# One list of steps for the first block of a fused chunk attention and Mish feed-forward kernel

## The chip, the core and the metric

The kernel runs on one NeuronCore of a Trainium2 chip. The metric is device time in microseconds (us). The kernel before takes 855.69 us (median of 3 runs, 854.79 to 856.61).

The engines that matter here: PE (TensorE, matrix products into PSUM), ACT (ScalarE, tables, copies and casts), DVE (VectorE, arithmetic on tensors), and SP (SyncE, whose queue issues nearly all transfers). Each engine takes its own instructions strictly in the order in which the program states them, and waits on semaphores for the others.

## The reference

```python
# attention, apart for each chunk of 64 positions; q, k, v: (8 batch, 8 heads, 576, 64)
scores = (q_c @ k_c.T) / sqrt(64)
attn   = exp(scores - max(scores))
attn   = attn / (sum(attn) + 1e-9)
x      = (attn @ v_c)                 # -> (4608 tokens, 512)
# feed-forward
h   = x @ w_in                        # 512 -> 2048
g   = h * tanh(log1p(exp(min(h, 20))))   # Mish
out = g @ w_out                       # 2048 -> 512
```

The two weights come as 64-bit floats; a matrix product in single precision is made here of products of a rounded upper part ("hi") and a rest ("lo").

## The kernel before, in words

The 4608 tokens are 36 tiles of 128. The first block holds four of them (two "pairs" of tiles, 512 tokens); the other 32 follow in four groups of four pairs (m = 1 to 4). These groups use products of sums of sub-matrices; their operands are 256 KB pieces of the weights, kept in DRAM. Only the first block works with the weights as they come in. It has to do four things at once:

- **Attention of its own tokens** (pairs 0 and 1), in halves of one tile: scores (`a_scores`, PE), `a_max`, `a_sub` (DVE), `a_exp` (ACT), `a_inverse` and `a_norm` (DVE), `a_transpose` (PE), `a_copy` (ACT), `a_values` (PE), and the split of the result into hi and lo (`a_hi` on ACT, `a_lo` on DVE, tile `x_first`).
- **Attention of the next group** (pairs 2 to 5), the same steps on whole pairs; `a_raw` (ACT) keeps the result, and `x_step` (ACT and DVE) makes the split operands of the group m = 1 of it.
- **The weights.** There are 19 loads: 0 to 5 bring one row of 128 columns (0.5 MB of doubles), 6 to 18 bring two (1 MB). Below, "load n" is the transfer (L102), "scale n" its two ACT steps (L114, L119), "bits n" its two DVE steps (L132), "hi n" the ACT cast (L150) and "lo n" the DVE subtraction (L153). Even n from 6 on are `w_in` (tile `wi`), odd ones `w_out` (tile `wo`). Bits of `w_in` also go to DRAM (L136, `cs`). The tile that the loads fill (`wst`) and the tile of the scaled values (`wc`) have four places: a load of two rows takes two of them, so load n can go out when bits n-2 are done, and scale n can begin when load n has landed and lo n-2 has freed the place in `wc`.
- **The feed-forward of the block.** Slot s (0 to 15) is a strip of 128 of the 2048 hidden columns. `up s` (L461) is 12 products of 512 columns, Mish (L474, "mish s") goes to a tile `z`, `gh s` and `gl s` split it, `down s` (L493) is 12 products that add to four accumulators over all slots. Two banks hold the results of `up`, so `up s` needs mish s-2.

When both strips of a `wi` tile are there, `w_keep(u)` (L163) stores three quarters of it to DRAM, three transfers of 256 KB ("keep u", u = 0 to 7), for the products of the groups. After the last lo, `s_load`, `s_adds`, `s_hi`, `s_lo` build the four other operands of unit 0 from `cs`: they use the place of the whole `wc` tile, so they wait for lo 18, and their store (L200) must land before the third product of unit 0 can load its operand (L751).

What sets the order before: `prologue` (attention of the first tokens, loads 0 to 6, up 0 to 1) is written out by hand with loops over halves; then `slot(s)` states one slot of the feed-forward with the steps of one load, in a fixed pattern; and two small tables (`on_pe`, `beside_pe`) hang the attention of the next pairs, the x steps and the sums onto half slots. In a slot, `up s+1` comes first, then load, hi, the split of z, scale, lo, then `down s-1`, mish, bits, keep. Which casts `gh` go to ACT is in `BY_SCALAR`. The unit code of the groups follows, and reads the last two `down` groups from a list.

Of the kernel before, what the change touches and what calls it, by code (L numbers as in the profile page):

```python
# [23 lines left out]
def kernel(  # L24
# [451 lines left out]
    def g_split(d, z, name, on_scalar=False):  # L476
        d["gh"] = ew.tile([P, TOK], F32R, name=f"gh_{name}", tag="gh")
        if on_scalar:
            nc.scalar.copy(out=d["gh"], in_=z)
# [3 lines left out]
        nc.vector.tensor_tensor(out=d["gl"], in0=z, in1=d["gh"].bitcast(F32), op=ALU.subtract)
# [5 lines left out]
    def down_mm(key, f, d, t, n):  # L489
        if f == 0 and n == 0:  # L490
            acc[t] = ps_o.tile([P, DM], F32, name=f"o_{key}_{t}", tag=f"o{t}")
        g, part = ((d["gl"], 0), (d["gh"], 1), (d["gh"], 0))[n]
        nc.tensor.matmul(  # L493
            acc[t],
            lhsT=g[:, t * P : (t + 1) * P],
            rhs=wo[:, f, part],
            start=(f == 0 and n == 0),
            stop=(f == NF - 1 and n == 2),
        )
# [118 lines left out]
    on_pe, beside_pe = {}, {}
    for i, (h0, h1) in enumerate(((2, 8), (10, 15), (17, 22), (24, 28))):
        j = first_pair(1) + i  # L620
        for n, step in ((0, a_scores), (h1 - h0, a_transpose), (h1 - h0 + 1, a_values)):
            on_pe.setdefault(h0 + n, []).append((step, j))
        for n, steps_ in (
            (0, (load_v,)),
            (1, (a_max, a_sub)),
            (2 - (i == 3), (a_exp,)),
            (3 - (i == 3), (a_inverse,)),
            (4 - (i == 3), (a_norm,)),
            (h1 - h0, (a_copy,)),
            (h1 - h0 + 1, (a_raw,)),  # L630
        ):
            beside_pe.setdefault(h0 + n, []).extend((step, j) for step in steps_)
        if i:
            beside_pe.setdefault(h0 - 6, []).append((lambda j: load_qk(j, pool=(xo_p, "x")), j))
    for s, half, steps_ in (
        (19, 0, (0,)),
        (20, 0, (1,)),
        (21, 0, (2,)),
        (22, 0, (3, 4)),
        (27, 0, (5, 6)),  # L640
        (28, 0, (7, 8)),
        (29, 0, (9, 10)),
        (30, 1, (0, 1)),
        (31, 1, (3, 4, 2, 5, 7)),
    ):
        beside_pe.setdefault(s, []).extend((lambda n, half=half: x_step(1, half, n), n) for n in steps_)

    beside_pe[27].append((s_adds, 0))
    beside_pe[28].append((s_hi, 0))
    beside_pe[29].insert(0, (s_lo, 0))  # L650
    beside_pe[30].append((s_load, 1))

# [4 lines left out]
    BY_SCALAR = (1, 3, 5, 7, 8, 10, 12, 14)  # L657

    def slot(s):
        n = s + SINGLE - 1  # L660
# [9 lines left out]
        if s == 1:  # L670
            w("lo", now)
        w("scale", 5 if s == 0 else n + 1)
        if s == 0:
            w("bits", 4)
        if s != 1:
            w("lo", now)
        run(beside_pe, 2 * s)

        if s < NF - 1:
            filled()  # L680
        down(0, s, it[s])
        run(on_pe, 2 * s + 1)
        if s + 1 < NF:
            it[s + 1]["z"] = z_tile(f"z_{s + 1}")
            mish(it[s + 1]["z"], it[s + 1]["h"])
        if s == 0:
            w("hi", 4)
            w("bits", 5)
            w("load", SINGLE + 1)
            w("lo", 4)  # L690
            w("scale", SINGLE)
            w("bits", SINGLE)
        elif s == 1:
            w("hi", n)
            w("lo", n)
# [5 lines left out]
        if s == NF - 3:
            s_load(0)
            load_op()
            load_op()
        run(beside_pe, 2 * s + 1)
        if s == NF - 2:
# [494 lines left out]
```

## Time and profile before

| | |
|---|---|
| median of 3 runs | 855.69 us |
| profiled execution, its time | 854.58 us |
| its span, first to last instruction | 852.8 us |
| granted TensorE clock, mean | 0.988 |
| up 1 ends, up 2 begins on PE | 31.6 us |
| down 14 begins (the last `down` before unit 0) | 142.6 us |
| third product of unit 0 (first with an operand built in this block) | 151.7 us |

The first block is the stretch from 0 to about 145 us. From about 190 us on PE works nearly without a pause (each 20 us from 200 to 300 us hold 20.00 us of PE work), so what the first block takes is nearly a constant ahead of the rest. A busy share is the share of time in which an engine works at all; the clock that PE is granted is shown as a number from 0 to 1; the DMA share is the mean busy share of the 16 DMA engines. In a row of the timeline or of a group, the text in brackets is how long the engine sat idle just before, and what ended that.

### The profile page before, as it was taken

The page shows a single profiled execution, that of the slowest core. Times are in us where ns is not written, and L with a number is a line of the kernel's source. Part 1 is how long each engine was busy: PE and PEld are TensorE (multiplying, and loading weights), DVE is VectorE, ACT ScalarE, POOL GpSimd, SP SyncE. Part 2 cuts the span into 40 slices and gives each one's busy share as a digit, 9 for nine tenths or more (in the row PEclk, how much of TensorE's full clock was granted, in tenths as well). Part 3 has the DMA queues.
Part 4 walks back from the last instruction along what each step waited for, and adds up shares of the span by engine and source line. Part 5 has one row for each costly group of instructions (what it writes and reads, how often), then busy time and mean ns, then how long its engine had stood idle before and what let it go on. Part 6 is the DMA issues. An engine that isn't in the chain of part 4 may idle for free.

```text
span 852.8 us, 15933 instructions
## 1 busy us (share of the span) xinstructions
PE 810.4 (95%) x6300; PEld 686.4 (80%) x6300; DVE 521.6 (61%) x765; ACT 436.1 (51%) x640; POOL 0.7 (0%) x6
## 2 busy tenths in 40 slices
PE   4878989889999999999999999999999999999997
PEld 3756867568888888788888888877899988889997
DVE  6787889655564663665764764444788723347663
ACT  4667875444443552543543534555656534444443
POOL 0000000000000000000000000000000000000000
PEclk9988999999999999999999999999999999999999
DMA  7698883877758411788886227876567777666773
GB/s 284 238 318 291 279 282 138 263 247 268 270 204 279 111 51 57 230 286 287 258 279 212 73 99 254 301 226 184 159 164 222 216 230 195 189 195 175 209 197 88
DMA packets 96441, 181.40 MB, mean 213 GB/s; under 512 B 9072, under 2 KB 29552, under 8 KB 94320
## 3 DMA queue, kind: packets, MB, share of 16 engines
q1 hardware_dynamic: 95936, 179.74, 66.4%
q8 instruction: 50, 0.82, 0.4%
q10 hardware_dynamic: 432, 0.66, 0.2%
q14 instruction: 23, 0.19, 0.1%
HBM read 137.36 MB, written 42.99 MB: 211 GB/s over the span
## 4 chain that ended last, share of the span: by engine, by line
PE 76%; DVE 10%; DMA 5%; ACT 5%; issue 2%; SPq 1%; DVEq 0%; ACTq 0%
PE x L764 17%; PE X L1063 9%; PE v L764 9%; PE Z L1063 5%; PE y L764 5%; PE av L271 2%; DMA wst<-in_w_in 2%; PE s L271 2%; PE h L461 2%; PE o L493 2%; PE pt L339 2%; DVE wc L132 1%; PE Y L1063 1%; PE o_(1, 1)_0_2761 L493 1%; PE o_(2, 1)_0_4413 L493 1%
## 5 line engine op out<-in xcount | busy, mean ns | idle before, releaser
L764 PE MATMUL x<-x_T,w 128*128 128x512 f32 x576 | 144.7, 394 | 6.4 <-ACT zb L869 3.1
L764 PEld LDWEIGHTS x<-x_T,w 128*128 128x128 f32 x576 | 106.2, 188 | 33.3 <-ACT zb L869 4.4
L1028 ACT CAST gh<-G 128x512 fp32r<-128x512 f32 x96 | 58.8, 621 | 59.4 <-PE X L1063 32.4
L1030 DVE TENSOR_TENSOR gl<-G,gh 128x512 fp32r<-128x512 f32 x96 | 65.1, 688 | 37.3 <-ACT gh L1028 36.1
L1063 PE MATMUL X<-w,gh 128*128 128x256 f32 x512 | 72.3, 283 | 0.0
L1063 PEld LDWEIGHTS X<-w,gh 128*128 128x128 f32 x512 | 66.3, 192 | 0.2
L474 ACT ACTIVATE G<-G 128x512 f32<-128x512 f32 x48 | 30.3, 632 | 57.4 <-DVE G L776 57.4
L776 DVE TENSOR_TENSOR G<-v,G 128x512 f32<-128x512 f32 x32 | 21.9, 689 | 57.2 <-ACT G L1008 34.7
L461 PE MATMUL h<-x_first,wi 128*128 128x512 f32 (+1 forms) x204 | 49.3, 393 | 1.7 <-ACT wi L150 0.8
L764 PE MATMUL v<-x_B,w 128*128 128x512 f32 x192 | 48.8, 393 | 1.3 <-DVE zb L776 1.3
L474 ACT ACTIVATE zb<-zb 128x512 f32<-128x512 f32 x32 | 20.2, 632 | 58.0 <-DVE zb L776 58.0
L764 PE MATMUL x<-x_B,w 128*128 128x512 f32 x192 | 48.6, 394 | 0.8 <-DVE x_B L416 0.8
L764 PE MATMUL y<-x_B,w 128*128 128x512 f32 x192 | 49.1, 397 | 0.0
L764 PE MATMUL v<-x_T,w 128*128 128x512 f32 x192 | 47.6, 390 | 1.2 <-DMA w<-wa 1.2
L461 PEld LDWEIGHTS h<-x_first,wi 128*128 128x128 f32 x204 | 37.7, 195 | 10.3 <-ACT wi L150 1.2
L764 PEld LDWEIGHTS v<-x_B,w 128*128 128x128 f32 x192 | 35.5, 188 | 9.9 <-DVE zb L776 2.6
L764 PEld LDWEIGHTS v<-x_T,w 128*128 128x128 f32 x192 | 35.9, 188 | 9.3 <-issue 1.6
L1063 PE MATMUL X<-w,gl 128*128 128x256 f32 x256 | 41.8, 284 | 1.3 <-DVE gl L1030 1.2
L764 PEld LDWEIGHTS x<-x_B,w 128*128 128x128 f32 x192 | 35.2, 188 | 8.6 <-DVE x_B L416 1.2
L493 PE MATMUL o<-wo,gh 128*128 128x512 f32 x128 | 41.8, 407 | 0.3 <-DVE wo L153 0.3
L764 PEld LDWEIGHTS y<-x_B,w 128*128 128x128 f32 x192 | 35.1, 188 | 7.7
L481 DVE CAST gh<-z 128x512 fp32r<-128x512 f32 x40 | 16.9, 423 | 39.7 <-PE o_(2, 0)_3_3328 L493 20.6
(181 smaller groups left out, 1583.5 us busy)
## 6 DMA issues: line engine op xcount, KB each, us to landing
w<-wa SPq DMA_DIRECT2D x224, 256.0 KB, 3.2
w<-wb SPq DMA_DIRECT2D x112, 256.0 KB, 2.9
v<-in_v SPq DMA_DIRECT2D x16, 512.0 KB, 5.7
wa<-a SPq DMA_DIRECT2D x8, 1024.0 KB, 4.3
wb<-t SPq DMA_DIRECT2D x8, 1024.0 KB, 5.0
wst<-in_w_out SPq DMA_DIRECT2D x7, 1024.0 KB, 6.5
wst<-in_w_in SPq DMA_DIRECT2D x6, 1024.0 KB, 6.0
wa<-wi SPq DMA_DIRECT2D x24, 256.0 KB, 3.7
```

The costliest lines, as they stand in the source:

```text
L132: nc.vector.scalar_tensor_tensor(out=c, in0=x, scalar=mask, in1=y, op0=op, op1=ALU.bitwise_or)
L271: nc.tensor.matmul(o[h * CHUNK : (h + 1) * CHUNK, c, t - ts.start, g], lhsT=l[rows, t, 2 * g + h], rhs=r[rows, t, 2 * g + h], start=True, ...
L339: nc.tensor.transpose(out=d["pt", ts.start][:, t - ts.start, g], in_=d["p"][:, t, g].rearrange("p c k -> p (c k)"), identity=ident,)
L461: nc.tensor.matmul(h[:, cols], lhsT=wi[i // 2][:, i % 2, w_, kt], rhs=x[:, x_, kt, cols], start=(n == 0), stop=(n == 3 * NK - 1),)
L474: nc.scalar.activation(out=out_, in_=in_, func=AF.Mish)
L481: nc.vector.tensor_copy(out=d["gh"], in_=z)
L493: nc.tensor.matmul(acc[t], lhsT=g[:, t * P : (t + 1) * P], rhs=wo[:, f, part], start=(f == 0 and n == 0), stop=(f == NF - 1 and n == 2),)
L764: nc.tensor.matmul(o, lhsT=t[:, w_, kt], rhs=x[x_][:, kt], start=(start and i == 0), stop=(i == 5), skip_group_check=not start,)
L776: nc.vector.tensor_tensor(out=z, in0=o, in1=z, op=ALU.add)
L1028: nc.scalar.copy(out=d["gh"], in_=g)
L1030: nc.vector.tensor_tensor(out=d["gl"], in0=g, in1=d["gh"].bitcast(F32), op=ALU.subtract)
L1063: nc.tensor.matmul(o, lhsT=d[g][:, t * P : (t + 1) * P], rhs=w_[:, part], start=(k in (0, 1, 3) and u == 0 and t % 2 == 0 and n == 0), sto ...
```

## The change

All steps of the first block now stand in one list, `ORDER`, which `first_block()` goes through from left to right; `atom()` turns a word into the call. The steps and their sizes are the same. What differs:

- the order of nearly everything, on every engine;
- the first tokens' attention interleaves its two halves, and its tiles are placed in other banks (`TOP_ATTENTION`, places `h`, `0`, `2`); load 0 and load 1 go out behind q and k of pair 1, loads 2 and 3 and `v` of pair 1 behind the first store of bits;
- `gh` and `gl` can stand apart (`g_upper`, `g_lower`), and seven casts `gh` instead of eight are on ACT;
- two `up` are stated in a row at several places (3 and 4, 7 and 8, 14 and 15), with two `down` in a row behind;
- the stores "keep u" stand behind the next load instead of ahead of it, and keep 4 comes after load 16, keep 6 after load 17, keep 5 and 7 after load 18.

```diff
-    def prologue(ps_f):
...
-        load_qk(0, None, (FIRST, SECOND), (nc.sync, nc.scalar))
-        w("load", 0)
-        load_v(0, room[0])
-        load_qk(1, (room[1], room[2]), (FIRST, SECOND))
-        w("load", 1)
-        load_v(1, room[3])
-        w("load", 2)
-        w("load", 3)
...
-    BY_SCALAR = (1, 3, 5, 7, 8, 10, 12, 14)
-
-    def slot(s):
...
-            up(s + 1, last="w")
-        run(on_pe, 2 * s)
-        if s > 0:
-            w("load", n + 2)
-        now = (3, 5, n)[min(s, 2)]
-        w("hi", now)
-        g_split(it[s], it[s]["z"], f"0_{s}", s in BY_SCALAR)
...
-            w("bits", n + 1)
-        if s % 2 == 0:
-            w_keep(s // 2)
...
+    ORDER = """
+        rooms, qk0, v0, qk1, a_scores 0 0, a_max 0 0, a_sub 0 0, a_scores 0 1, a_max 0 1,
...
+        a_inverse 0 1, a_norm 0 1, a_T 0 1, a_copy 0 0, a_V 0 0, a_copy 0 1, load 1, bits 0,
+        load 2, load 3, v1, hi 0, lo 0, a_hi 0 0, a_scores 1 0, a_V 0 1, a_hi 0 1, a_lo 0 0,
...
+        bits 5, lo 3, load 7, keep 0, mish 1, hi 4, gh 1, lo 4, hi 5, scale 6, bits 6, open,
+        fill 0, scores 0, up 2, lo 5, max 0, fill 1, mish 2, gh 2, sub 0, scale 7, bits 7,
+        load 8, load_v 0, load 9, hi 6, keep 1, hi 7, lo 6, scale 8, exp 0, lo 7, up 3, gl 1,
+        mish 3, up 4, gl 2, bits 8, load 10, inverse 0, load_qk 1, fill 2, gh 3, fill 3, norm 0,
+        gl 3, scale 9, mish 4, bits 9, load 11, hi 8, lo 8, up 5, keep 2, mish 5, T 0, copy 0,
...
+        load_v 2, raw 1, fill 8, scores 2, fill 9, mish 9, bits 14, load 16, up 10, hi 14, gh 9,
+        max 2, sub 2, gl 9, fill 10, scale 15, lo 14, ops 2, keep 4, exp 2, bits 15, load 17,
+        keep 6, load_qk 3, mish 10, up 11, gh 10, gl 10, hi 15, lo 15, fill 11, up 12,
...
+        keep 7, max 3, sub 3, exp 3, bits 18, fill 12, fill 13, gh 13, gl 13, hi 18, lo 18,
+        s_load 0, inverse 3, norm 3, up 14, up 15, mish 14, mish 15, gh 14, x 0 6, x 0 8,
...
+    BY_SCALAR = (2, 5, 7, 11, 12, 13, 14,)
+
+    def atom(name, *args):
...
+        elif name == "fill":
+            if a < NF - 1:
+                filled()
+            down(0, a, it[a])
...
+    def first_block():
+        for step in ORDER.split(","):
+            name, *args = step.split()
+            atom(name, *map(int, args))
```

In `ORDER`, "fill k" emits down k-1 and notes down k; "scores", "T", "V" with one number are the attention of the pairs 2 to 5 (numbers 0 to 3); "x h n" is step n of half h.

Three places show how instructions move. The first is SP's queue around loads 10 to 12 (the rows `wst`) of the program before; `cs` is the store of bits, `wa` the keep, `qk` and `v` are attention inputs.

```order
L136 DMA cs_118<-wc 128x1024
L163 DMA wa_100<-wi_390 128x2x256 x3
L102 DMA wst<-in_w_in 128x2x1024
L102 DMA wst<-in_w_out 128x2x1024
L136 DMA cs_119<-wc 128x1024
L163 DMA wa_101<-wi_537 128x2x256 x3
L102 DMA wst<-in_w_in 128x2x1024
```

The same place in the changed program:

```order
L136 DMA cs_118<-wc 128x1024
L102 DMA wst<-in_w_in 128x2x1024
L254 DMA qk_595<-in_q 128x2x512
L254 DMA qk_595<-in_k 128x2x512
L102 DMA wst<-in_w_out 128x2x1024
L163 DMA wa_101<-wi_544 128x2x256 x3
L136 DMA cs_119<-wc 128x1024
L102 DMA wst<-in_w_in 128x2x1024
```

Each even load now follows its store of bits directly; the three transfers of a keep follow the odd load.

The second place is DVE between bits 6 and bits 8 (L132 on 1024 elements; L153 is lo, L297 and L309 are max and sub of pair 2, L481 and L483 are gh and gl). Before:

```order
L132 SCALAR_TENSOR_TENSOR wc<-wst,wc 128x1024
L483 TENSOR_TENSOR gl_1_512<-z_447,gh_1_510 128x512
L153 TENSOR_TENSOR wo<-wc,wo 128x512
L153 TENSOR_TENSOR wi_537<-wc,wi_537 128x2x512
L132 SCALAR_TENSOR_TENSOR wc<-wc,wst 128x1024
L132 SCALAR_TENSOR_TENSOR wc<-wst,wc 128x1024
L297 TENSOR_REDUCE m_0_542<-s_0_475 128x16
L309 TENSOR_TENSOR p_544<-s_0_475,m_0_542 128x2x8x64
L481 CAST gh_2_561<-z_535 128x512
L483 TENSOR_TENSOR gl_2_563<-z_535,gh_2_561 128x512
L153 TENSOR_TENSOR wo<-wc,wo 128x2x512
```

Changed (gh and gl are now L485 and L489):

```order
L132 SCALAR_TENSOR_TENSOR wc<-wst,wc 128x1024
L153 TENSOR_TENSOR wo<-wc,wo 128x512
L297 TENSOR_REDUCE m_0_512<-s_0_465 128x16
L309 TENSOR_TENSOR p_534<-s_0_465,m_0_512 128x2x8x64
L132 SCALAR_TENSOR_TENSOR wc<-wc,wst 128x1024
L132 SCALAR_TENSOR_TENSOR wc<-wst,wc 128x1024
L153 TENSOR_TENSOR wi_544<-wc,wi_544 128x2x512
L153 TENSOR_TENSOR wo<-wc,wo 128x2x512
L489 TENSOR_TENSOR gl_1_568<-z_449,gh_1_452 128x512
L489 TENSOR_TENSOR gl_2_585<-z_530,gh_2_532 128x512
```

lo 5 moves ahead of gl 1, max and sub move ahead of bits 7, lo 6 behind it, and gl 1 comes seven instructions later, beside gl 2, whose gh has gone to ACT.

The third place is PE at the same time (L461 is up, one row of 12 products; L493 is down, of which the first accumulator of each is shown). Before, up 3, down 1, up 4, down 2:

```order
L461 MATMUL h_546<-x_first,wi_390 128x512 x12
L493 MATMUL o_0_519<-wo,gl_1_512 128x512
L493 MATMUL o_0_519<-wo,gh_1_510 128x512 x2
...
L461 MATMUL h_596<-x_first,wi_537 128x512 x12
L493 MATMUL o_0_519<-wo,gl_2_563 128x512
L493 MATMUL o_0_519<-wo,gh_2_561 128x512 x2
```

Changed, up 3, up 4, down 1, down 2 (down is now L499):

```order
L461 MATMUL h_555<-x_first,wi_400 128x512 x12
L461 MATMUL h_572<-x_first,wi_544 128x512 x12
L499 MATMUL o_0_514<-wo,gl_1_568 128x512
L499 MATMUL o_0_514<-wo,gh_1_452 128x512 x2
...
L499 MATMUL o_0_514<-wo,gl_2_585 128x512
L499 MATMUL o_0_514<-wo,gh_2_532 128x512 x2
```

up 4 has moved ahead of down 1.

More of the change, by code (lines that the diff above doesn't have):

```diff
@@ L476, in g_split, with g_upper @@
     def g_split(d, z, name, on_scalar=False):
+        g_upper(d, z, name, on_scalar)
+        g_lower(d, z, name)
+    def g_upper(d, z, name, on_scalar):
         d["gh"] = ew.tile([P, TOK], F32R, name=f"gh_{name}", tag="gh")
@@ L618 @@
[L618 to L651, printed above, removed]
@@ L655, in run @@
             step(arg)
-    BY_SCALAR = (1, 3, 5, 7, 8, 10, 12, 14)
-    def slot(s):
-        n = s + SINGLE - 1
-        if 1 <= s and s + 1 < NF:
-            up(s + 1, last="w")
-        run(on_pe, 2 * s)
-        if s > 0:
-            w("load", n + 2)
-        now = (3, 5, n)[min(s, 2)]
-        w("hi", now)
-        g_split(it[s], it[s]["z"], f"0_{s}", s in BY_SCALAR)
[L670 to L695, printed above, removed]
-            w("bits", n + 1)
-        else:
-            w("bits", n + 1)
-        if s % 2 == 0:
-            w_keep(s // 2)
[L701 to L706, printed above, removed]
-            for i in range(LOOK - 2):
-                load_op()
@@ new lines, with room, open_accumulators @@
+    A, B = slice(0, PTOK), slice(PTOK, TOK)
+    first = ExitStack()
+    ps_f = first.enter_context(tc.tile_pool(name="ps_f", bufs=1, space=bass.MemoryType.PSUM))
+    PLACES = {"h": HOME, "0": (ps_f, "o0"), "2": (ps_f, "o2")}
+    rooms = {}
+    opened = {}
+    def room(n):
+        if n not in rooms:
+            rooms[n] = xo_p.tile([P, 2, 2, H, CHUNK], F32, name=f"room_{n}", tag="x")
+        return rooms[n]
+    def open_accumulators():
+        first.close()
+        opened["o"] = ctx.enter_context(tc.tile_pool(name="ps_o", bufs=1, space=bass.MemoryType.PSUM))
@@ new lines @@
+    """
+    BY_SCALAR = (2, 5, 7, 11, 12, 13, 14,)
+    def atom(name, *args):
+        if name in TOP:
+            return TOP[name]()
+        a = args[0]
+        j = first_pair(1) + a
+        if name in TOP_ATTENTION:
+            step, places = TOP_ATTENTION[name]
+            t = args[1]
+            kw = {} if places is None else {"place": PLACES[places[a][t]]}
+            step(a, (FIRST, SECOND)[t], **kw)
+        elif name in steps:
+            steps[name](a)
+        elif name in attention:
+            attention[name](j)
+        elif name == "up":
+            up(a, last="w")
+        elif name == "gh":
+            g_upper(it[a], it[a]["z"], f"0_{a}", a in BY_SCALAR)
+        elif name == "gl":
+            g_lower(it[a], it[a]["z"], f"0_{a}")
+        elif name == "fill":
+            if a < NF - 1:
+                filled()
+            down(0, a, it[a])
+        elif name == "mish":
+            it[a]["z"] = z_tile(f"z_{a}")
+            mish(it[a]["z"], it[a]["h"])
+        elif name == "keep":
+            w_keep(a)
+        elif name == "x":
+            x_step(1, *args)
+        elif name == "ops":
+            for _ in range(a):
+                load_op()
+        else:
+            {"s_load": s_load, "s_adds": s_adds, "s_hi": s_hi, "s_lo": s_lo}[name](a)
@@ new lines @@
+    attention = {
+        "scores": a_scores,
+        "load_v": load_v,
+        "max": a_max,
+        "sub": a_sub,
+        "exp": a_exp,
+        "inverse": a_inverse,
+        "norm": a_norm,
+        "T": a_transpose,
+        "copy": a_copy,
+        "V": a_values,
+        "raw": a_raw,
+        "load_qk": lambda j: load_qk(j, pool=(xo_p, "x")),
+    }
+    def first_block():
+        for step in ORDER.split(","):
+            name, *args = step.split()
+            atom(name, *map(int, args))
@@ L1136 @@
     with tc.manual_schedule():
-        with tc.tile_pool(name="ps_f", bufs=1, space=bass.MemoryType.PSUM) as ps_f:
-            prologue(ps_f)
-        ps_o = ctx.enter_context(tc.tile_pool(name="ps_o", bufs=1, space=bass.MemoryType.PSUM))
-        for s in range(NF):
-            slot(s)
+        first_block()
         for m in range(1, BOTH_FROM):
```

103 lines of the change are left out of this document (43 added, 60 removed).

## The prediction

> **What bounds the kernel now.** I read the page first, then the stretches of the first block, then the chain of waits through it.
>
> ```profile
> PEclk9988999999999999999999999999999999999999
> ```
>
> (40 slices of 21.3 us each.) Only the first slices show a lowered clock, the sign that PE waited long. So the change is worth what it takes off the first 150 us, and the rest follows shifted.
>
> ```profile
> 0.00:31.56 31.56, 17.38 (x308) 14.59 (x308) 21.63 (x39) 17.55 (x29) 0.70 (x6) 0.95 0.70 253
> 31.56:137.60 106.04, 93.59 (x796) 74.42 (x796) 86.26 (x97) 76.67 (x87) 0.00 (x0) 0.92 0.76 269
> 64.82:124.30 59.48, 53.25 (x515) 43.56 (x516) 46.91 (x51) 46.33 (x52) 0.00 (x0) 0.91 0.83 292
> 39.60:124.30 84.70, 72.87 (x591) 57.88 (x590) 67.85 (x74) 62.26 (x69) 0.00 (x0) 0.90 0.84 296
> ```
>
> The columns are the stretch, its length, busy time of PE, of weight loading, DVE, ACT and POOL with their counts, granted clock, DMA share, GB/s. No engine is full: between 31.56 and 137.60 DVE works 86.26 of 106.04 us, DMA is at 0.76. The chain says why:
>
> ```profile
> 30.14 5.28 DMA wst<-in_w_in
> 41.51 1.13 ACT wc L114
> 52.08 1.22 DVE wo L153
> 58.34 6.37 DMA wst<-in_w_in
> 69.88 4.98 PE h L461 x12
> 137.56 6.09 DMA wa<-wi
> ```
>
> (start, duration, what.) It runs over loads 6 and 10, over ACT and DVE steps of the weights in between, and at the end over keep 7. Each engine waits in turn for the others. What PE pays:
>
> ```profile
> 21.40 0.63 PE L339 MATMUL pt<-ident,p 128*128 128x128 f32 x4 [2.98 <-ACT wst L119]
> 24.18 1.99 PE L271 MATMUL av<-ps,room 64*64 64x64 f32 x64
> 31.58 3.01 PE L461 MATMUL h<-x_first,wi 128*128 128x512 f32 x12 [0.26 <-ACT z L474]
> 52.31 0.77 PE L493 MATMUL o<-wo,gl 128*128 128x512 f32 x1 [4.17 <-DVE gl L483]
> 57.72 2.90 PE L461 MATMUL h<-x_first,wi 128*128 128x512 f32 x12
> 67.89 1.98 PE L271 MATMUL av<-ps,v 64*64 64x64 f32 x64 [3.37 <-ACT ps L349]
> 69.81 5.05 PE L461 MATMUL h<-x_first,wi 128*128 128x512 f32 x12
> 84.17 2.88 PE L461 MATMUL h<-x_first,wi 128*128 128x512 f32 x12
> 115.50 1.94 PE L339 MATMUL pt<-ident,p 128*128 128x128 f32 x8 [3.16 <-DVE p L330]
> 142.58 0.50 PE L493 MATMUL o<-wo,gl 128*128 128x512 f32 x1
> ```
>
> The row at 31.58 is up 2, the last one the start of down 14. From one to the other PE has 14 up and 14 down, at 2.72 us when warm (start to next start around 84.17), and four attentions at about 3.0: 88.2 us of work in 111.0. The excess is 22.8 us. Stalls of 3.2 to 4.2 us are each followed by a slow group: 12 products in 5.05 us instead of 2.88.
>
> **The change, part by part.** Work is the same but for one `gh` that moves from ACT to DVE, so every term is a shift of a wait. I walk the new order by hand with these durations:
>
> ```profile
> L132 DVE SCALAR_TENSOR_TENSOR wc<-wst,wc 128x1024 uint32<-128x1024 uint32 x13 | 15.9, 1225 | 0.4
> L114 ACT ACTIVATE wc<-wst 128x1024 f32<-128x1024 f32 x13 | 14.9, 1145 | 6.4 <-DMA wst<-in_w_in 3.7 <-DVE wo L153 2.8
> L150 ACT CAST wo<-wc 128x1024 fp32r<-128x1024 f32 x7 | 7.3, 1049 | 8.1 <-DVE wc L132 8.1
> L153 DVE TENSOR_TENSOR wo<-wc,wo 128x1024 fp32r<-128x1024 f32 x7 | 8.5, 1221 | 1.1 <-ACT wo L150 1.0
> L483 DVE TENSOR_TENSOR gl<-z,gh 128x512 fp32r<-128x512 f32 x14 | 9.7, 692 | 9.1 <-ACT gh L479 8.9
> wst<-in_w_out SPq DMA_DIRECT2D x7, 1024.0 KB, 6.5
> DMA to landing us min/median/max: 3.7/6.2/8.8
> ```
>
> Neighbours overlap a little, so in a row of them a scale takes 2.05 us, bits 2.4, hi 0.95, lo 1.14, gl 0.61.
>
> *Start, to up 1: +0.3.* Loads 2, 3 and `v` of pair 1 now queue on SP behind the store of bits 0.
>
> ```profile
> 7.27 0.33 SPq L102 DMA_DIRECT2D wst<-in_w_in  x1
> 13.68 0.33 SPq L136 DMA_DIRECT2D cs<-wc  x1
> ```
>
> Load 2 went at 7.27 and goes at about 15. That queue holds up only loads and `v`; `v` needs about 7 us and is wanted by the values of pair 1, at 24.18 before. Load 0 moves behind 2 MB of q, k and v and lands near 12, so scale 0 delays one copy by about 0.9 us, and the copies already wait for DVE. Ends: 0, if all of it is hidden, to +2, if `v` lands at 26. I take +0.3, since DVE's stream stays full.
>
> *To scale 10: −6.0, with that 0.3 in it.* Load 6 goes out behind bits 3 as before and lands near 35.2. Scale 6 and bits 6 end at 39.6. lo 5 is now next on DVE, at 40.3, and scale 7, which had waited 2.8 us for it, starts there instead of at 41.51. Then hi 6 ends at 43.4, max and sub of pair 2 fill DVE to 42.6, bits 7 to 44.9, lo 6 and lo 7 to 47.2, gl 1 and gl 2 to 48.4. Before, lo 7 ran from 52.08 to 53.3. PE waits 2.7 us ahead of up 4 (from 40.7), then does down 1 and down 2 by 53.3; before, they were done at 57.72, where up 5 begins. Scale 8 starts at 46.1, bits 8 end at 50.9.
>
> ```profile
> 55.72 0.34 SPq L136 DMA_DIRECT2D cs<-wc  x1
> 56.10 2.14 SPq L163 DMA_DIRECT2D wa<-wi  x3
> 64.82 1.13 ACT L114 ACTIVATE wc<-wst 128x1024 f32<-128x1024 f32 x1 [0.78 <-DMA wst<-in_w_in]
> ```
>
> Before, load 10 went 2.6 us after its `cs` store, since the three transfers of the keep took 2.14 us of the queue. Now it follows at once, at 51.2, and lands at 57.7; by then lo 8 (58.4 by DVE's list: inverse, gh 3, norm, gl 3, bits 9, lo 8) is last, and scale 10 starts at 58.8 for 64.82.
>
> *Scale 10 to scale 18: −7.2.* In the new order DVE's list from lo 9 to lo 17 holds 9 lo, 8 bits, 5 gh, 9 gl, two attentions (max, sub, inverse and norm, each the size of a lo step, and 0.4 of small ones), three x splits and two x differences: 10.3 + 19.2 + 2.3 + 5.5 + 10.4 + 1.8 + 1.3 = 50.8 us. The rows of before show 46.91 us busy in 59.48. Walked through, the new list waits 1.5 us, so scale 18 comes 52.3 us after scale 10, at 111.1. The two waits for norm and copy that stopped PE at 67.89 and 115.50 shrink, because copy 0 now stands ahead of scale 10 on ACT and norm 2 ahead of lo 16 on DVE.
>
> ```profile
> 124.30 1.16 ACT L114 ACTIVATE wc<-wst 128x1024 f32<-128x1024 f32 x1
> ```
>
> *Scale 18 to the third product of unit 0: −2.1.*
>
> ```profile
> 134.74 0.65 SPq L177 DMA_DIRECT2D a<-cs  x1
> 143.61 0.33 SPq L200 DMA_DIRECT2D wa<-a  x1
> 147.94 1.28 SPq L751 DMA_DIRECT2D w<-wa  x3
> 151.69 1.66 PE L764 MATMUL x<-x_T,w 128*128 128x512 f32 x6 [0.93 <-ACT z L825]
> ```
>
> Before, 27.4 us: 10.4 to the load from `cs`, 8.9 to the store L200, 4.3 until the operand can load, 3.7 to the product; beside it the x splits waited until 143.65 for keep 7. Now keep 5 and 7 go before lo 18 and land under it. The chain is scale 2.05, bits and hi behind exp and DVE 6.2, lo to the load 1.0, and then the same links less about 1 us of DVE queue, 25.3 us. From this product on the unit repeats the chain `a<-cs`, L200, operand of the next units, all shifted.
>
> Sum of the walk: −6.0 − 7.2 − 2.1 = −15.3.
>
> *What the walk leaves out.* First, **transfers**. From 39.6 on it must move what 39.60:124.30 moved, 296 GB/s × 84.7 us = 25.1 MB, less one keep of 0.8, so 24.3 MB, in 71.5 us. A share of 1 would be 296/0.84 = 352 GB/s and 69.0 us, so the walk asks for a share of 0.97. At the share of before it takes 82.1 us. I take the middle, 0.92, 75.0 us: **+3.5**; ends 0 and +10.6. Second, the **clock**: the 2.7 us gap ahead of up 4.
>
> ```profile
> 22.00:24.00 2.00, 0.86 (x5) 0.72 (x4) 1.90 (x5) 0.59 (x1) 0.00 (x0) 0.75 0.00 0
> ```
>
> Behind the 2.98 us gap at 21.40 the clock fell to 0.75. A cold group costs 5.05 − 2.88 = 2.2 us, but here ACT and DVE, not PE, set the chain; ends 0 and 2.2, I take **+0.7**. [...]
>
> −15.3 + 3.5 + 0.7 = −11.1. The profiled execution took 854.58, which gives 843.5; the median of the runs is 855.69, which gives **844.6**.
>
> **The rivals.**
>
> 1. *The DMA engines follow.* Then the walk holds, −15.3 and up to 3 us more where x steps move off the tail: 838 to 841. For it: loads alone ran above 400 GB/s in short stretches, and part of the 0.84 before was queue held by late bits, not rate.
>
> ```profile
> 78.00:82.00 4.00, 4.00 (x19) 3.30 (x19) 3.93 (x6) 3.81 (x5) 0.00 (x0) 1.00 1.06 406
> ```
>
> [...] Against: the mean with stores in it was 296 at 0.84.
>
> 2. *The rate stays.* Transfers take 82.1 us from 39.6, load 18 lands at 121.7 for about 124.3: −2.6, with the −2.1 behind it −4.7: 851.
>
> 3. *Slower: loads land late.* The keeps now go right behind an odd load, so the next loads share the DMA engines with them. The walk stands up to landings of 6 to 8.4 us, load by load. At the maximum of before, 8.8, the delays (2.4, 1.2, 0.4, 2.8, 1.6, 1.4, 0.1, 2.8, 1.1 for loads 8, 10, 12 to 18) add up to 13.8 if none hides another, which leaves −1.5. From there each further 1 us on nine loads costs up to 9 us, and the doubled up, which puts PE idle with a ready down behind it, adds a cold group of 2.2 at up 4, up 8 and up 15. At 9 us: −1.5 + 1.8 + 6.6 less 3 that hides, about +4: 860. Against: 6.2 is the median, and 8.8 one load.
>
> 4. *The shift is lost behind the block.* The units' waits on `a<-cs`, L200 and the operands would have to hang on something that did not move. In the rows at 134.74 to 151.69 each link begins with the one ahead of it, and the first with lo 18, so I see nothing that stays: 855.7.
>
> **How the numbers follow.** The forecast (841 to 849) has 0.50, rival 1 0.20, rival 2 0.15, rival 3 0.10, rival 4 0.05. The predicted time is 844.6. About 0.2% (1.7 us) is what a measurement here can tell from no change. Faster: 0.50 + 0.20 + most of 0.15 and a little of the rest, 0.83; same 0.06; slower 0.11. Range: low at rival 1's floor, 838; high at 855.5, which leaves out rival 3, and half of rival 4.
>
> **What would show it.** Right: load 10 issued within 1 us of its `cs` store and near 51; scale 10 near 59 to 61; scale 18 at 111 to 116; DVE idle under 8 us between them; DMA share above 0.88 from 40 to 110; down 14 near 130. Wrong: rows "scale waits for DMA" of more than 2 us at many loads (rivals 2 and 3), the clock below 0.9 in more slices than before, or values of pair 1 waiting for `v` (start). If all of the shift is there at 190 us but the span is not shorter, rival 4.

## The result, and the profile after

The changed kernel takes **842.88 us** (median of 4 runs, 841.59 to 843.93) where the kernel before took 855.81 beside it (4 runs, 854.79 to 856.61): a ratio of 0.985, 95% interval 0.983 to 0.987. The forecast was 844.6. The profiled execution took 843.93 us with a span of 842.1; against the profile of before (854.58, span 852.8) that is 10.7 us, while the medians differ by 12.9. The last section but two returns to those 2 us.

| us from the span's start | before | forecast | after |
|---|---|---|---|
| scale 6 | 35.53 | | 36.49 |
| scale 7 | 41.51 | 40.3 | 42.34 |
| scale 10 | 64.82 | 58.8 | 61.24 |
| scale 18 | 124.30 | 111.1 (walk), 115.3 with transfers and clock | 118.64 |
| third product of unit 0 | 151.69 | 136.4 (walk), 140.6 | 143.73 |
| a later product of that unit, `v<-x_B` | 162.13 | | 151.71 |

The stretches of the first block in the changed kernel (columns as in the prediction):

```profile
39.60:112.00 72.40, 66.97 (x536) 53.54 (x535) 65.09 (x73) 57.51 (x64) 0.00 (x0) 1.00 0.96 331
61.24:118.64 57.40, 53.06 (x591) 42.87 (x590) 51.08 (x58) 44.14 (x51) 0.00 (x0) 1.00 0.95 329
```

Before, 39.60:124.30 had the DMA engines at 0.84 and 296 GB/s and the clock at 0.90. Now they are busy 0.96 of the time, at 331 GB/s, and PE holds its full clock (1.00): none of the stalls of 3 to 4 us is left. The same loads now land later (the row of a transfer: count, size, median us from issue to landing; from the first 140 us of the changed kernel):

```profile
wst<-in_w_out SPq DMA_DIRECT2D x7, 1024.0 KB, 8.0
wa<-wi SPq DMA_DIRECT2D x24, 256.0 KB, 8.4
```

Before, the first row had 6.5, and the keeps:

```profile
wa<-wi SPq DMA_DIRECT2D x24, 256.0 KB, 3.7
```

SP's queue, ACT and PE of the changed kernel:

```profile
52.96 0.33 SPq L136 DMA_DIRECT2D cs<-wc  x1
53.40 0.37 SPq L102 DMA_DIRECT2D wst<-in_w_in  x1
...
126.36 0.65 SPq L177 DMA_DIRECT2D a<-cs  x1
134.65 0.34 SPq L200 DMA_DIRECT2D wa<-a  x1
```

```profile
34.97 0.60 ACT L474 ACTIVATE z<-h 128x512 f32<-128x512 f32 x1 [0.90 <-PE h L461]
36.49 1.13 ACT L114 ACTIVATE wc<-wst 128x1024 f32<-128x1024 f32 x1
41.82 0.62 ACT L483 CAST gh<-z 128x512 fp32r<-128x512 f32 x1 [2.18 <-PE o L499]
42.34 1.12 ACT L114 ACTIVATE wc<-wst 128x1024 f32<-128x1024 f32 x1
61.24 1.15 ACT L114 ACTIVATE wc<-wst 128x1024 f32<-128x1024 f32 x1
82.02 1.15 ACT L114 ACTIVATE wc<-wst 128x1024 f32<-128x1024 f32 x1 [2.21 <-DMA wst<-in_w_out]
118.64 1.12 ACT L114 ACTIVATE wc<-wst 128x1024 f32<-128x1024 f32 x1 [1.84 <-DMA wst<-in_w_out]
```

```profile
27.71 7.22 PE L461 MATMUL h<-x_first,wi 128*128 128x256 f32 x24 [0.70 <-ACT x_first L379]
45.46 2.14 PE L461 MATMUL h<-x_first,wi 128*128 128x512 f32 x8 [1.01 <-ACT wi L150]
134.21 0.50 PE L499 MATMUL o<-wo,gl 128*128 128x512 f32 x1
143.73 1.63 PE L748 MATMUL x<-x_T,w 128*128 128x512 f32 x6 [1.98 <-DMA w<-wa]
151.71 1.65 PE L748 MATMUL v<-x_B,w 128*128 128x512 f32 x6
```

Load 10 leaves 0.44 us behind its store of bits (2.6 before). The first PE row is a surprise: up 0B and up 1, 24 products, took 7.22 us; in the profile of before these took 4.44. Their lateness runs on: mish 1 waits 0.90 us on ACT for up 1, and scale 6 stands behind it; down 0, which frees the buffer of `gh 2`, comes late, `gh 2` waits 2.18 us for it on ACT, and scale 7 stands right behind. The ACT rows at 82.02 and 118.64 are scale 13 and scale 18, the only two after scale 6 that wait for their loads.

The chain of waits is no longer a zigzag over loads and weight steps. From 49.99 to about 128 us it runs mostly over PE, with one load in it, and then over DVE and ACT:

```profile
49.99 5.76 PE o L499 x24
...
73.36 8.58 DMA wst<-in_w_out
...
122.74 5.45 PE h L461 x24
```

### The profile page after: what moved, and what is told of

It is laid out like the page before. It is cut to its first block, busy times and chain, and to the rows that moved or that the text cites. A ratio compares the mean times of both kernels' runs of the same rounds, so it can differ in the third digit from the quotient of the medians.

```text
span 842.1 us, 15938 instructions
## 1 busy us (share of the span) xinstructions
PE 806.2 (96%) x6300; PEld 684.1 (81%) x6300; DVE 521.7 (62%) x766; ACT 435.5 (52%) x639; POOL 0.7 (0%) x6
## 4 chain that ended last, share of the span: by engine, by line
PE 80%; DVE 9%; ACT 4%; DMA 3%; issue 2%; SPq 1%; DVEq 0%; ACTq 0%
PE x L748 18%; PE X L1047 9%; PE v L748 9%; PE Z L1047 5%; PE y L748 5%; PE h L461 4%; PE o L499 3%; PE s L271 2%; PE av L271 2%; PE pt L339 1%; PE Y L1047 1%; PE o_(1, 1)_0_2761 L499 1%; PE o_(2, 1)_0_4413 L499 1%; PE o_(2, 1)_1_4417 L499 1%; PE o_(1, 1)_1_2765 L499 1%
## 5 line engine op out<-in xcount | busy, mean ns | idle before, releaser
L1012 ACT CAST gh<-G 128x512 fp32r<-128x512 f32 x96 | 58.8, 621 | 59.4 <-PE X L1047 32.3
L461 PE MATMUL h<-x_first,wi 128*128 128x512 f32 (+1 forms) x204 | 49.9, 399 | 2.4 <-ACT wi L150 1.0
L461 PEld LDWEIGHTS h<-x_first,wi 128*128 128x128 f32 x204 | 38.5, 202 | 10.9 <-ACT wi L150 1.4
L485 DVE CAST gh<-z 128x512 fp32r<-128x512 f32 x41 | 17.3, 423 | 39.5 <-PE o_(2, 0)_3_3328 L499 20.6
L499 PE MATMUL o<-wo,gh 128*128 128x512 f32 x128 | 39.8, 390 | 0.0
```

The costliest lines, as they stand in the source:

```text
L461: nc.tensor.matmul(h[:, cols], lhsT=wi[i // 2][:, i % 2, w_, kt], rhs=x[:, x_, kt, cols], start=(n == 0), stop=(n == 3 * NK - 1),)
L499: nc.tensor.matmul(acc[t], lhsT=g[:, t * P : (t + 1) * P], rhs=wo[:, f, part], start=(f == 0 and n == 0), stop=(f == NF - 1 and n == 2),)
L1012: nc.scalar.copy(out=d["gh"], in_=g)
```

## The experiments

The theory after the result: the new lists of ACT, DVE and PE give most of the gain, the stores behind the loads the rest, the start nothing, and transfers limit what is left. The rivals: the store order alone does it, or the start; or transfers are hidden. All kernels are the list form of one of the two programs with steps moved, but for two that store less and one that adds work; scale 10, scale 18 and the third product are read as in the table above.

### Which part of the change

Four kernels: the old start (up to `mish 0` and load 6) with the new rest, the new start with the old rest, and the keeps alone put back, or alone moved.

```diff
 oldstart_newrest:  ORDER = the steps of prologue() + all of the new list that is not among them
 newstart_oldrest:  ORDER = the new order of prologue()'s steps + the old slots, old BY_SCALAR
 new_keeps_ahead (the same for keep 0 and 2 to 5 and loads 8, 12, 14, 16, 18):
-  bits 8, load 10, ... load 11, hi 8, lo 8, up 5, keep 2
-  load 9, hi 6, keep 1
+  load 9, hi 6
+  bits 8, keep 1, load 10
 old_keeps_late (the same for keep 0, 2, 3, 4, 6; keep 5 behind load_v 3):
-  mish 3, bits 8, keep 1, inverse 0
+  up 3, load 9, keep 1, hi 7
```

> The changed list from bits 4 and mish 0 on, behind the start of before (loads 2, 3 and v of pair 1 early, both halves in the old order). My theory: the gain lies in the rest of the list, and the new start costs about 1 us, since its 24 products of up 0 and up 1 ran cold (7.22 us for 4.44) and scale 6 began at 36.5 instead of 35.5. So 841 to 842.5, about 1 us faster than the changed kernel. Rival: the rest of the list presupposes the new start (pair 2's q and k early), then 844 to 847.

> The changed start, and the old order from there on. My theory: the start alone gains nothing and costs about 1 us: 856 to 857. Rival: the start carries part of the gain (pair 2's q and k and load 4 fill the hole in the transfers from 17 to 24 us): 850 to 853.

> The changed list with keep 0 to 5 put back ahead of loads 8, 10, 12, 14, 16 and 18, keep 6 and 7 as changed. Theory A (the engines' lists carry the gain, the place of the stores only a part): each load waits 2 us of SP's queue, transfers in all are the same, 845 to 848. Theory B (the place of the stores is the gain): 851 to 856.

> The old order with keep 0 to 3 behind loads 7, 9, 11, 13, keep 4 and 6 behind loads 16 and 17, keep 5 behind the v of the last pair; all else as before. Theory A: 851 to 854, loads 10 and 16 go out about 2 us sooner and little else changes. Theory B: 844 to 848.

Measured, 5 rounds, the kernel before at 855.33 beside them:

| | time (us) | ratio to before, interval | profiled execution | scale 10 | scale 18 | third product |
|---|---|---|---|---|---|---|
| old start, new rest | 843.24 | 0.986 (0.985 to 0.988) | 843.65 | 62.85 | 117.15 | 144.15 |
| new start, old rest | 855.91 | 1.001 (1.000 to 1.002) | 856.71 | 67.30 | 126.96 | 154.81 |
| new, keeps ahead | 846.22 | 0.990 (0.988 to 0.991) | 850.87 | 62.98 | 123.49 | 148.35 |
| old, keeps late | 852.33 | 0.997 (0.995 to 0.998) | 850.63 | 64.53 | 121.94 | 149.34 |

The last four columns are of one execution each. For "new, keeps ahead" that one took 4.7 us more than the median and for "old, keeps late" 1.7 less, so the worth of a part is read from the medians. The start is worth nothing by itself; the expectation that the old one would be 1 us faster missed. The lists without the new order of keep 0 to 5 give 9.1 us (855.33 − 846.22), the store order without the new lists 3.0; the sum, 12.1, is nearly the whole 12.9, so no interaction of the two shows. With the keep ahead, the queue and the keep's own landing look as before:

```profile
54.53 0.34 SPq L136 DMA_DIRECT2D cs<-wc  x1
54.91 2.06 SPq L163 DMA_DIRECT2D wa<-wi  x3
57.08 0.64 SPq L102 DMA_DIRECT2D wst<-in_w_in  x1
```

```profile
wa<-wi SPq DMA_DIRECT2D x24, 256.0 KB, 4.3
```

So a keep that lands in 4.3 us ahead of a load lands in 8.4 behind it, where nobody is waiting for it, and the load gains the 2.1 us of queue.

### What the transfers cost

Each keep stores one of its three pieces, and the groups' products take that piece for the other two.

```diff
-        for n, (f, a) in enumerate(((0, 0), (0, 1), (1, 1))):
+        for n, (f, a) in enumerate(((0, 0),)):
             nc.sync.dma_start(out=ops_of[u][:, n], in_=t[:, f, :, a])
...
-    nc.sync.dma_start(out=t.bitcast(F32), in_=src[u][:, place])
+    nc.sync.dma_start(out=t.bitcast(F32), in_=src[u][:, 0 if src is ops_of and place < 3 else place])
```

> The changed list, but each keep stores one of its three pieces, and the operand loads of the groups take that piece for the other two: the result is not the reference's, the work of the engines and the operand loads are the same, and 4.2 MB of stores are gone from the first block. Theory A1 (transfers bound the changed kernel from 40 to 112 us: share 0.96): scale 10 to scale 18 falls from 57.4 to 52 to 54 us, the engines' own lists, and the time to 836 to 839. Rival (the lists bound it already, the full share is only early queueing): 841.5 to 843.5.

> The same cut in the order of before, result not the reference's for the same reason. Theory A1: before was bound by its lists and its queue, not by transfers (share 0.84), so it gains what a keep holds SP ahead of a load, 1.4 us at a few loads: 850 to 853. Rival (before was bound by transfers too): 844 to 848.

Measured (3 rounds, before 855.24): the new order 840.99 us, ratio 0.984 (0.980 to 0.987); the old order 851.45, 0.995 (0.993 to 0.997). In the new order, with the lighter traffic:

```profile
60.37 1.16 ACT L114 ACTIVATE wc<-wst 128x1024 f32<-128x1024 f32 x1
113.75 1.15 ACT L114 ACTIVATE wc<-wst 128x1024 f32<-128x1024 f32 x1
```

```profile
40.00:110.00 70.00, 66.31 (x534) 53.37 (x534) 64.90 (x72) 58.54 (x65) 0.00 (x0) 1.00 0.88 301
```

Scale 10 to 18 takes 53.4 us in place of 57.4, near the 52.3 that the walk had for a load that is never late. So full transfers cost 4.0 us in that stretch. On ACT they are the waits of scale 13 and scale 18 for their loads, 2.21 and 1.84 us, 4.05 together; with the lighter traffic no scale after the first has such a wait. Of these about 2 reach the end by the medians (842.88 to 840.99, with intervals that overlap), 3.2 by the profiled spans (842.1 to 838.9, the first of an execution 1.1 us above its median). In the old order the lighter traffic gives 3.8 us, little more than the 3.0 of moving the keeps alone; these two runs do not part the queue from the traffic there.

### The doubled up

```diff
-  mish 3, up 4, gl 2, bits 8, ... load_qk 1, fill 2, gh 3
+  mish 3, gl 2, bits 8, ... load_qk 1, fill 2, up 4, gh 3
-  up 7, up 8, mish 7, ... fill 6, gh 7
+  up 7, mish 7, ... fill 6, up 8, gh 7
```

> The changed list with up 4 behind down 1 and up 8 behind down 5, as before. Theory A: PE is not what is late there, no change within 1 us: 842 to 844. Rival of the prediction (the doubled up leaves PE idle with a down ready): 838 to 841.

Measured (5 rounds): 846.16 us (844.36 to 847.83), ratio 0.988 (0.986 to 0.991). The expectation of no change missed: it is 3.3 us slower by the medians (1.1 by the profiled spans, 843.2 for 842.1). The interval just touches the changed kernel's (0.983 to 0.987), so the sign is likely and the size open. PE and ACT of this kernel:

```profile
41.17 2.88 PE L461 MATMUL h<-x_first,wi 128*128 128x512 f32 x12
49.68 0.76 PE L499 MATMUL o<-wo,gl 128*128 128x512 f32 x1 [5.62 <-DVE gl L489]
...
54.31 2.89 PE L461 MATMUL h<-x_first,wi 128*128 128x512 f32 x12
...
59.76 2.88 PE L461 MATMUL h<-x_first,wi 128*128 128x512 f32 x12
```

```profile
62.73 0.60 ACT L474 ACTIVATE z<-h 128x512 f32<-128x512 f32 x1 [3.92 <-issue]
...
65.41 1.16 ACT L114 ACTIVATE wc<-wst 128x1024 f32<-128x1024 f32 x1
```

The PE rows with 12 products are up 3, up 4, up 5. Behind up 3 PE waits 5.62 us for `gl 1`, since down 1 is next. In the changed kernel up 4 stands there and fills the wait (pieces of 1.01, 0.59 and 0.61 us are left of it), and up 5 comes at 55.59. Here up 5 ends at 62.64. On ACT mish 5 starts at 62.73 after 3.92 us of idle time; its row names no releaser, but its input is what up 5 writes. And `copy 0`, `hi 9` and scale 10 stand behind mish 5: scale 10 slips by 4.2 us. Of these 0.9 are left at scale 18 (119.57) and 2.4 at the third product (146.08), which waits there for an x split. The prediction had the doubled up only as a danger (a cold group of 2.2 us each); by this run it is one of the places where the gain comes from.

### DVE between bits 6 and bits 8

```diff
-  up 2, lo 5, max 0, fill 1, mish 2, gh 2, sub 0, scale 7, bits 7, load 8, load_v 0,
-  load 9, hi 6, keep 1, hi 7, lo 6, scale 8, exp 0, lo 7, up 3, gl 1, mish 3, up 4, gl 2, bits 8
+  up 2, gl 1, lo 5, fill 1, mish 2, gh 2, scale 7, hi 6, lo 6, bits 7, max 0, sub 0, gl 2,
+  load 8, load_v 0, load 9, keep 1, hi 7, scale 8, exp 0, lo 7, up 3, mish 3, up 4, bits 8
```

> The changed list with one place as in the kernel before: on DVE between bits 6 and bits 8, gl 1 stands ahead of lo 5, max and sub of pair 2 behind bits 7, lo 6 ahead of bits 7. All else is as in the changed kernel. Theory (the engines' lists carry some 9 us of the gain, and the term up to scale 10 is this place): scale 7 waits for lo 5 again, scale 10 comes 1 to 3 us later than the 61.24 us of the changed kernel, and as transfers bind behind it about half of that stays: 843.5 to 845.5 us. Rival (transfers alone bind from 40 us on, the DVE order there is free): scale 10 within 0.5 us of 61.24, no change, 842.9 us.

Measured (5 rounds, before 855.71): 843.94 us (842.32 to 845.74), ratio 0.986 (0.984 to 0.989), which does not part from the changed kernel's 0.985. The profile says more:

```profile
48.91 1.05 ACT L150 CAST wo<-wc 128x1024 fp32r<-128x1024 f32 x1 [3.69 <-DVE wc L132]
49.86 1.12 ACT L114 ACTIVATE wc<-wst 128x1024 f32<-128x1024 f32 x1
...
62.96 1.15 ACT L114 ACTIVATE wc<-wst 128x1024 f32<-128x1024 f32 x1
...
118.28 1.13 ACT L114 ACTIVATE wc<-wst 128x1024 f32<-128x1024 f32 x1 [1.34 <-DMA wst<-in_w_out]
```

hi 7 waits 3.69 us for bits 7 again, as it did before the change, scale 8 comes 1.7 us later than the 48.16 of the changed kernel and so does scale 10. But at scale 18 nothing of it is left (118.28 for 118.64). The theory was right up to scale 10 and wrong behind it: a delay of 1.7 us is paid back where the transfers set the pace. It is still there at scale 12 (76.49 for 74.76) and gone at scale 13 (82.19 for 82.02), the one that waits 2.21 us for its load in the changed kernel. Of the 4.2 us of the up apart, 1.9 were left there (83.88).

### The tail

Three kernels: keep 6 and the first two operand loads behind load 18; that with bits 18, hi 18 and lo 18 ahead of the softmax of pair 5; keep 7 behind the load of the sums, as it was.

```diff
 new_keep6_late:
-  lo 14, ops 2, keep 4, exp 2, bits 15, load 17, keep 6, load_qk 3, ... load_v 3, raw 2,
-  ... keep 7, max 3
+  lo 14, keep 4, exp 2, bits 15, load 17, load_qk 3, ... load_v 3, keep 6, raw 2,
+  ... keep 7, ops 2, max 3
 new_lo18_first, in addition:
-  max 3, sub 3, exp 3, bits 18, fill 12, fill 13, gh 13, gl 13, hi 18, lo 18, s_load 0
+  bits 18, max 3, hi 18, lo 18, s_load 0, sub 3, exp 3, fill 12, fill 13, gh 13, gl 13
 new_keep7_late:
-  keep 5, keep 7, max 3, ... lo 18, s_load 0, inverse 3
+  keep 5, max 3, ... lo 18, s_load 0, keep 7, inverse 3
```

> The changed list with keep 6 and the first two operand loads of unit 0 also moved behind load 18 (1.3 MB less ahead of it). Theory A1: load 18 lands 2 to 4 us sooner, of which the chain to the third product of unit 0 keeps 1 to 2.5: 840 to 842. Rival: they only move into the way of the load from cs and of the store of the sums: 843 to 845.

> The changed list with keep 6 and the first two operand loads behind load 18 (alone they moved scale 18 1.65 us earlier and the time not at all), and now also bits 18, hi 18 and lo 18 ahead of sub and exp of pair 5 (bits 18 ahead of its max too). Theory (DVE's list behind scale 18 swallowed that 1.65 us): the load from cs goes out at 123 to 124.5 us instead of 126.4, the third product of unit 0 comes 1 to 2 us earlier than 143.73, the time is 840.5 to 842.5 us. Rival (DVE is full from 126 to 141 us, so whatever comes sooner there makes the x splits later): third product within 0.7 us, 842.5 to 843.5 us.

> The changed list with one step moved: keep 7 goes out behind the load of the sums (s_load 0), as in the kernel before, instead of ahead of bits 18's cast. Theory (what the tail won is the DVE list; keep 7 would land near 131 us and is first wanted near 136): no change within 1 us, 842 to 844 us. Rival (the tail's 2 us came from keep 5 and 7 landing under lo 18): the third product of unit 0 comes 2 us later than 143.73, and the time is 845 us.

Measured: 842.98 us (ratio 0.985, 0.983 to 0.987), 843.70 (0.985, 0.983 to 0.987) and 842.06 (0.985, 0.982 to 0.988): no change in any of them. The first moved scale 18 to 116.99 and the load from `cs` only to 126.11, so the 1.65 us were lost in DVE's list in between. The second takes that away, and the load does go out early:

```profile
123.52 0.65 SPq L177 DMA_DIRECT2D a<-cs  x1
135.14 0.33 SPq L200 DMA_DIRECT2D wa<-a  x1
```

```profile
130.96 1.80 DVE L189 TENSOR_TENSOR a<-a 128x256 f32<-128x256 f32 x4
```

2.84 us earlier than in the changed kernel, but the sums (L189), which it feeds, start on DVE 0.48 us later than there (130.96 for 130.48), and the third product comes at 144.39. The rival holds: from 126 on DVE is the limit. Its busy time in the changed kernel:

```profile
126.00:141.00 15.00, 13.66 (x122) 10.71 (x121) 14.61 (x25) 9.94 (x17) 0.00 (x0) 1.00 0.31 113
```

14.61 of 15.00 us. What is won ahead of it only waits there. keep 7 behind the load leaves 8.82 us from that load to L200 (8.29 in the changed kernel), half a microsecond at most, and nothing in the time. Its third product comes at 145.03 in the profiled execution (845.28 us, the median is 842.06), but DVE was already 1.5 us late at lo 17 (118.34 for 116.83), ahead of the step that was moved. It does not bring the old place back: keep 7 goes out at 128.02, in the kernel before at 136.57.

### A warm start

24 transposes of the identity are added at six places between up 0A and up 0B, into the bank that up 1 fills later; nothing reads them.

```diff
+    def warm():
+        if 1 not in it:
+            it[1] = {"h": ps_h.tile([P, TOK], F32, name="h_1", tag="h")}
+        for _ in range(4):
+            nc.tensor.transpose(out=it[1]["h"][:, 0:P], in_=ident, identity=ident)
...
-  up0A, a_sub 1 0, ... a_T 1 0, a_copy 1 0, ... a_T 1 1, a_copy 1 1, a_V 1 1, load_qk 0
+  up0A, warm, warm, warm, a_sub 1 0, ... a_T 1 0, warm, a_copy 1 0, ... a_T 1 1, warm,
+  a_copy 1 1, a_V 1 1, warm, load_qk 0
```

> The changed list with work added: 24 transposes of the identity (four at each of six places: three behind up 0A, one each behind a_T 1 0, a_T 1 1 and a_V 1 1) into the bank that up 1 fills later, so that PE sits idle for shorter stretches between 20 and 27 us; nothing reads them. Theory (the 24 products of up 0B and up 1 ran 7.22 us instead of 4.44 because PE had idled): they take 4.4 to 4.8 us, mish 0 comes 2 us earlier, scale 6 under 1 us earlier, and as transfers bind from 40 us on the time is 842.0 to 842.9 us, with a smaller spread. Rival (the slow group does not come from these gaps): still 6.4 us or more, 842.9 us or up to 0.5 more.

Measured (4 runs): **840.93 us** (838.40 to 841.55), ratio 0.982 (0.980 to 0.984), the lowest of all kernels that do the full work, below both the kernel before and the changed one. The interval still touches the changed kernel's (0.983 to 0.987), so the gain of 2 us over it is likely, not settled. The profiled execution took 838.40:

```profile
26.27 4.82 PE L461 MATMUL h<-x_first,wi 128*128 128x256 f32 x24 [0.21 <-ACT x_first L379]
```

```profile
34.15 1.15 ACT L114 ACTIVATE wc<-wst 128x1024 f32<-128x1024 f32 x1
39.64 1.12 ACT L114 ACTIVATE wc<-wst 128x1024 f32<-128x1024 f32 x1 [1.07 <-DMA wst<-in_w_out]
58.53 1.14 ACT L114 ACTIVATE wc<-wst 128x1024 f32<-128x1024 f32 x1
113.96 1.12 ACT L114 ACTIVATE wc<-wst 128x1024 f32<-128x1024 f32 x1 [1.72 <-DMA wst<-in_w_out]
```

```profile
40.00:110.00 70.00, 65.10 (x586) 52.03 (x585) 64.94 (x72) 58.17 (x64) 0.00 (x0) 1.00 0.98 346
```

The slow group is gone (4.82 us), and scale 6, 7 and 10 come 2.3 to 2.7 us earlier than in the changed kernel, scale 18 and the third product (139.07) 4.7 us. The profile is 2.5 us below its median and the changed kernel's 1.1 above, so these differences are larger than that of the medians. I had expected under 1 us of it to be left at scale 6, and that transfers would take the rest; instead the transfers followed, at a share of 0.98 and 346 GB/s.

## Why the prediction was right, and where not

- **Sign and size.** 844.6 was forecast with a net of −11.1; the profiled executions differ by −10.7, the medians by −12.9. The size is in part luck: at the third product −11.1 was forecast and −8.0 came, and 2.4 us that the sum did not have came behind it. Scale 10 (61.24) and scale 18 (118.64) lie outside the signs named for them (59 to 61, 111 to 116).
- **Start, +0.3.** Nothing in the time, as forecast (old start 843.24, new start with the old rest 855.91 beside 855.33). `v` of pair 1 came in time. But up 1, where this term ends, came 3.6 us later (34.93 for 31.32) and not 0 to 2: 0.8 is the later begin of up 0B, 2.8 the cold group; 1.0 of it is left at scale 6 (36.49 for 35.53). The profile of before, which gave the walk its durations, had run this stretch warm, and the three other profiles with the old start (6.45 us for the 24 products in the one with the new rest) ran it cold.
- **To scale 10, −6.0: measured −3.6.** Load 10 leaves 0.44 us behind `cs` and lo 6, lo 7 and both gl stand as walked, but 2 us later, because scale 7 did not start at 40.3. lo 5 ended at 41.75, 1.4 us late, since scale 6 stood behind mish 1, which waited for up 1; then `gh 2`, ahead of scale 7 on ACT, waited until 41.82 for down 0. Both come from the cold group (7.22 us for 4.44). The walk had no wait of ACT for PE here. With the warm start scale 10 comes at 58.53, near the forecast of 58.8, though from an earlier scale 6 (34.15; the walk has 35.2), so the stretch between them stays about 0.8 us longer than walked.
- **Scale 10 to 18, −7.2, with +3.5 for transfers: measured −2.1 where −3.7 stood.** The stretch is 57.4 us for 55.8. The walk (52.3) is nearly confirmed by the lighter traffic (53.4), and so is its DVE list: 51.08 us of work for the 50.8 walked, and 6.3 us of waits (57.40 − 51.08; under 8 was forecast). The transfers cost 4.0 and some more in place of 3.5, but not by the working behind the 3.5. The share was not 0.92 but 0.97 from 39.60 to 118.64, at which the 24.3 MB counted would take about 71 us and the term would be nothing; and that stretch moved more, 26.2 MB (331 GB/s × 79.04 us). Two errors made up for each other, which is luck. The cost came as two late loads, not as a mean rate. Of the 1.6 us that the stretch is longer than forecast, 0.5 is in the transfers' term (4.0 for 3.5, with a third of the keeps still there in that run) and 1.1 in the walk (53.4 for 52.3). Down 14, forecast near 130, begins at 134.21.
- **Clock, +0.7.** The gap ahead of up 4 cost nothing (the wait fell into three parts, and the clock stayed at 1.00 from 39.6 to 118.6). The clock was lost earlier, at up 0B and up 1, where the profile of before had the 24 products warm (4.44 us for 7.22); the term was of the right kind at the wrong place.
- **Scale 18 to the third product, −2.1: measured −2.3** (25.1 us for 27.4; 25.3 forecast). All of it lies ahead of the load from `cs`: 7.72 us from scale 18 to that load for 10.44 (about 9.3 walked), since max and sub of pair 5 now run while ACT scales. Behind it nothing was won (17.37 us to the product for 16.95; 16.0 walked), so the two halves missed in opposite directions. The reason given, keep 5 and 7 landing under lo 18, does not show: keep 7 behind the load changes nothing in the time, though it did not go out as late as before. DVE's list sets this stretch.
- **Behind it** another 2.4 us came that were not in the sum (−8.0 at the third product, −10.4 at the product now at 151.71). Between these two products PE had, before, waits of 0.95 and 1.40 us (and one of 0.18):

```profile
156.78 1.66 PE L764 MATMUL x<-x_T,w 128*128 128x512 f32 x6 [0.95 <-ACT zb L853]
160.29 1.66 PE L764 MATMUL x<-x_T,w 128*128 128x512 f32 x6 [1.40 <-ACT zb L869]
```

  of which the changed kernel has 0.22 us left. Rival 1's "up to 3 us more where x steps move off the tail" had it: the x split ahead of these steps on ACT stands 4.0 us before the third product (139.71), for 1.2 us before the change (150.54).
- **The rivals.** Rival 2 (the rate stays) fell with the share of 0.96. Rival 3 (loads land late) had the landings right in kind, 8.0 us for 6.5, which is where the walk is used up: of the nine loads in its list 13 and 18 came late, by 4.05 us in place of its 13.8. It had the price of the doubled up with the wrong sign, as far as the one run with it taken apart shows. Rival 4 fell: the shift arrives at the end in full.

Of the 2.3 us between the two differences, 10.7 and 12.9, 1.1 is the profile of after, above its median (843.93, 842.88), and 1.2 the profile of before, below its own (854.58, 855.81). The latter is the only one of the thirteen profiles without added transposes that has a short cold stretch at the start (3.4 us, where each of the others has at least 9). Whether that warm start made it faster is not shown: 10 of the 36 runs of before beside the experiments took less, and no run of before with its clock held cold or warm was made.

## What to carry to other kernels

Where engines with strict order wait for each other in turn, reorder by walking each engine's list, and let PE do a group that is ready in front of one whose operand is late (here up 4 in front of down 1, where PE else waited 5.62 us); put stores that nobody waits for behind the load that somebody waits for (a keep ahead of load 10 held SP's queue for 2.06 us). A walk from one profile inherits that profile's clock: look at the granted clock of a few executions before a duration is taken for fixed (the same 24 products took 4.44 us in one profile and 6.43 to 7.22 in nine others), and try to fill short gaps on PE where a cold stretch would sit on the chain (here a likely 2 us, not settled). A gain upstream counted here only up to what was full next: 1.7 us at scale 10 vanished in the loads (DMA share 0.95 from scale 10 to scale 18), and 2.8 at the tail vanished in DVE (14.61 of 15.00 us busy).
